# A segment-recurrent attention beside an MLP on one core: memory row subtracted, transposed scores in 128-token tiles, 512-token blocks, fixed instruction order

## The chip, the cores and the metric

One Trainium2 chip, one core of it. The metric is device microseconds (us) of one execution. Most executions of one kernel agree within 0.3%. All kernels quoted gave correct results.

Engine names as the profile has them: PE is TensorE (matmuls), PEld its weight loads, DVE is VectorE, ACT is ScalarE, POOL is GpSimd, SP is SyncE (here it only issues DMAs). A trailing q (SPq) is an engine's own queue. "L419" is line 419 of that kernel.

## The reference, cut to what matters

```python
x  = A_x                                   # [1, 2048, 1024] bf16
xn = layernorm(x)
return x + A(xn, ...) + B(xn, ...)

def A(x, mem0, Wq, Wk, Wv, Wo, seg_len):   # 64 segments of 32 tokens, 32 heads of 128, 8 memory rows
    mem = mem0
    for s in range(64):
        h = concat([mem, x[segment s]])                    # 40 rows
        q, k, v = h @ Wq, h @ Wk, h @ Wv
        p = softmax(mask(q @ k.T * scale))                 # memory rows and columns unmasked, rest causal
        o = (p @ v) @ Wo
        mem = o[:8]; outs.append(o[8:])                    # the next segment needs this one's memory
def B(x, w1, w2, w3, w4):
    h  = gelu(layernorm(x) @ w1)                           # 1024 -> 1024
    x1 = x + token_shift(h) @ w2                           # 1024 -> 1024
    return x1 + gelu(layernorm(x1) @ w3) @ w4              # 1024 -> 3584 -> 1024
```

Both kernels break the recurrence in the same way. After the first segment the eight memory rows of a segment are nearly equal, so one row per segment stands for all eight. All rows are guessed beforehand from segment means (the *speculation*), all segments are then computed in parallel, and at the end a *check* compares the computed memory rows with the guessed ones. Only if it fails does a slow serial loop run. It never ran here.

## The kernel before: the parts that the change and the argument touch

The stages in order: LayerNorm and w1 (first stage), w2 (second), w3 and w4 (third, with the speculation), attention with its output projection. A segment is 33 columns in attention: one copy of its memory row and 32 tokens. The memory key counts eight times by an additive 3.0 (a power of two) in the mask. Tiles hold three segments (99 columns), blocks twelve (396 columns).

```python
def attention(B, hg, QT, KTt, V):                       # four heads hg, one block
    for ti, (tok, T, msk) in enumerate(B["tiles"]):     # T = 99: three segments of 1 + 32
        for hh in range(4):
            nc.tensor.matmul(S3[:, hh, :], QT[:, hh, l0:l0 + T], KTt[:, hh, l0:l0 + T], start=True, stop=True)
        nc.vector.tensor_tensor(sm, S3, msk, op=ALU.add)            # 99 x 396
        nc.vector.tensor_reduce(mx, sm, op=ALU.max)
        nc.vector.tensor_tensor(sm, sm, mx, op=ALU.subtract)
        nc.scalar.activation(e, sm, ACTF.Exp, scale=LN2)
        nc.vector.tensor_reduce(ss, e, op=ALU.add)
        nc.vector.reciprocal(rs, ss)
        nc.vector.tensor_tensor(Pn, e, rs, op=ALU.mult)
        for hh in range(4):                                          # transpose on PE
            nc.tensor.matmul(T3[:, hh, :], Pn[:T, hh, :T], ident[:T, :T], start=True, stop=True)
        nc.scalar.copy(PT, T3)
        for hh in range(4):
            nc.tensor.matmul(O3[:, hh, :], V[:T, ti, ...], PT[:T, hh, :T], start=True, stop=True)
        nc.scalar.copy(oS[:, :, l0:l0 + T], O3)
# ... cut ...
for group in ((0,), (1,), (2,), (3,), (4, 5)):          # blocks of 12 segments, the last of 4
    for hg in range(8):
        # load wq, wk, wv (1 MB each); project Q, K over 396 columns, V over 384; attention
    out_proj(...)                                       # 32 matmuls of 512 columns per chain
```

The order of the instructions on each engine was left to the framework's scheduler: what stands after another in this text may run before it.

## Time and profile before

| | |
|---|---|
| time | 1677.18 us, median of 3 (1675.5 to 1679.21); 1676.58 with the fourth run that came with the result |
| span of the profiled run | 1674.9 us |
| first w3 matmul, first Q matmul | 163.1 us, 579.4 us |
| attention, first Q matmul to the end | 1095.5 us |

The first lines are from the page of the kernel before: busy time, share of the span and number of instructions by engine, then the share of each engine in the chain of work that ended last.

```profile
PE 1626.2 (97%) x10393; PEld 863.9 (52%) x10513; DVE 647.2 (39%) x1528; ACT 640.6 (38%) x1321; POOL 220.9 (13%) x380
...
PE 75%; DVE 10%; ACT 5%; DMA 4%; issue 3%; POOL 0%; SPq 0%; DVEq 0%; ACTq 0%; POOLq 0%
```

The next view tells for what PE waited: waiting line, releasing line, us in total, times, longest.

```profile
PE ps L233 <- ACT xn_160 L223: 10.9, 1, 10.9
PE ps L241 <- DVE xn2T L235: 5.4, 2, 4.3
PE psT L483 <- DVE Pn L479: 4.3, 14, 0.9
```

These waits add up to about 31 us, half of them at the start. The busy row leaves 48.7 us; the rest is the tail (5.8 us after PE's last matmul) and gaps too short for this view. In attention it waits 14 times for the softmax, never over 0.9 us. So PE's own instruction stream is the limit, and the question about any change is how many *slots* it takes from that stream. A busy PE hides this, because matmuls overlap: the mean record of a 512-column matmul is 379 ns long, yet one starts every 216 ns. Slots are read from starts. The following lines are from the timeline of PE: start, time from first start to last end, line, shapes, count.

```profile
519.27 1.29 PE L147 MATMUL ps<-xb,wv 128*128 128x71 bf16 x32
520.40 1.89 PE L338 MATMUL ps<-w_sb,h3T 128*128 128x512 bf16 x8
...
839.69 0.84 PE L419 MATMUL ps<-hTb,wk 128*128 128x396 bf16 x4
840.49 0.34 PE L489 MATMUL psO<-PT,V_7513 99*128 99x99 bf16 x4
840.83 0.39 PE L483 MATMUL psT<-c_ident_sb,Pn 99*99 99x99 bf16 x4
841.05 1.00 PE L419 MATMUL ps<-hTb,wk 128*128 128x396 bf16 x5
841.89 0.34 PE L489 MATMUL psO<-PT,V_7513 99*128 99x99 bf16 x4
842.07 1.51 PE L419 MATMUL ps<-hTb,wk 128*128 128x396 bf16 x8
843.42 5.34 PE L431 MATMUL ps<-wv,xTb 128*128 128x512 bf16 x23
```

Thirty-two matmuls of 71 columns take 520.40 - 519.27 = 1.13 us, so 35 ns each. From 839.69 to 843.42 are 3.73 us; 17 matmuls of 396 columns need 17 x 168 ns = 2.86 of them (168 ns is 10.75 us for 64 in a row), which leaves 73 ns for each of the 12 small ones of attention.

### The profile page before, as it was taken

Reading aid. Unit: us, or ns where it says so; the run is one execution under the profiler, and the core shown is the slowest. Engines: PE = TensorE matmul, PEld = TensorE weight load, DVE = VectorE, ACT = ScalarE, POOL = GpSimd, SP = SyncE. Lnnn points to the kernel's source line nnn. Section 1 sums busy time; section 2 is a strip of 40 time slices with the busy share of each in tenths; the row PEclk is TensorE's granted clock in tenths of the full one; section 3 lists DMA queues with packets and bytes.
Section 4 is the critical chain, followed back from the end, with each engine's and each line's share of the span. In section 5 each row is a group of like instructions: output and inputs, shape, how many; then the busy total and the mean of one; then the engine's idle time right before and its main releaser. Section 6 shows DMA issues by size and latency. Waiting matters only on the chain.

```text
span 1674.9 us, 26877 instructions
## 1 busy us (share of the span) xinstructions
PE 1626.2 (97%) x10393; PEld 863.9 (52%) x10513; DVE 647.2 (39%) x1528; ACT 640.6 (38%) x1321; POOL 220.9 (13%) x380
## 2 busy tenths in 40 slices
PE   6999999999999999999999999999999999999998
PEld 5544444444445455554555545554555546665643
DVE  8447000000101145552455505564255533465540
ACT  7635302112030044541455415553255514565520
POOL 4222011010200122220111101110011100101000
PEclk9999999999999999999999999999999999999999
DMA  6864421030309887552565526564365633445211
GB/s 243 327 201 166 176 65 62 32 95 1 120 7 341 301 293 244 175 173 72 178 189 178 165 86 194 178 190 141 116 193 172 183 95 118 138 129 152 65 45 46
DMA packets 202804, 252.95 MB, mean 151 GB/s; under 512 B 15691, under 2 KB 165400, under 8 KB 202672
## 3 DMA queue, kind: packets, MB, share of 16 engines
q1 hardware_dynamic: 186928, 217.25, 41.1%
q0 software_dynamic: 15744, 33.92, 5.7%
q8 instruction: 85, 1.39, 0.3%
q14 instruction: 47, 0.39, 0.1%
HBM read 204.11 MB, written 30.07 MB: 140 GB/s over the span
## 4 chain that ended last, share of the span: by engine, by line
PE 75%; DVE 10%; ACT 5%; DMA 4%; issue 3%; POOL 0%; SPq 0%; DVEq 0%; ACTq 0%; POOLq 0%
PE ps L419 16%; PE ps L431 13%; PE ps L317 11%; PE ps L362 11%; PE ps L338 11%; DVE Pn L479 3%; DVE ss L475 2%; PE psT L483 2%; PE psO L489 2%; PE ps L256 2%; ACT e L473 2%; PE psS L466 2%; DMA wv<-in_A_Wv_dram 1%; DVE sm L471 1%; DVE sm L468 1%
## 5 line engine op out<-in xcount | busy, mean ns | idle before, releaser
L419 PE MATMUL ps<-hTb,wk 128*128 128x396 bf16 (+2 forms) x1536 | 265.7, 313 | 0.0
L419 PE MATMUL ps<-hTb,wq 128*128 128x396 bf16 (+2 forms) x1536 | 263.5, 314 | 0.8 <-DVE Ro L339 0.8
L362 PE MATMUL ps<-wo_sb,oX 128*128 128x512 bf16 x998 | 226.4, 379 | 1.2
L431 PE MATMUL ps<-wv,xTb 128*128 128x512 bf16 x984 | 224.4, 379 | 2.1
L338 PE MATMUL ps<-w_sb,h3T 128*128 128x512 bf16 x876 | 194.9, 379 | 1.1
L317 PE MATMUL ps<-xn3T,w_sb 128*128 128x512 bf16 x876 | 193.3, 379 | 1.1
L468 DVE TENSOR_TENSOR sm<-psS,c_mask_reg_sb 99x396 f32<-99x396 f32 x160 | 87.4, 563 | 218.1 <-PE psS L466 218.1
L419 PEld LDWEIGHTS <-wq 128*128 128x128 bf16 x1536 | 133.7, 98 | 71.3 <-issue 1.1
L318 ACT ACTIVATE h3T<-ps 128x512 bf16<-128x512 f32 x112 | 66.6, 597 | 268.1 <-PE ps L317 213.7
L419 PEld LDWEIGHTS <-wk 128*128 128x128 bf16 x1536 | 131.4, 98 | 67.5
L431 PEld LDWEIGHTS <-xTb 128*128 128x128 bf16 x1024 | 99.9, 98 | 115.7
L362 PEld LDWEIGHTS <-oX 128*128 128x128 bf16 x1024 | 97.9, 98 | 112.1 <-DVE oX L492 1.6
L317 PEld LDWEIGHTS <-w_sb 128*128 128x128 bf16 x896 | 87.6, 98 | 105.2
L338 PEld LDWEIGHTS <-h3T 128*128 128x128 bf16 x896 | 86.9, 98 | 103.1
L432 ACT CAST Vp<-ps 128x512 bf16<-128x512 f32 x128 | 74.9, 585 | 151.4 <-PE ps L431 146.8
L485 ACT CAST PT<-psT 99x396 bf16<-99x396 f32 (+1 forms) x176 | 85.9, 488 | 63.4 <-PE psT L483 61.3
L475 DVE TENSOR_REDUCE ss<-e 99x4 f32<-99x396 f32 (+1 forms) x176 | 95.0, 545 | 23.4 <-ACT e L473 22.3
L479 DVE TENSOR_TENSOR Pn<-e,rs 99x396 bf16<-99x396 f32 (+1 forms) x176 | 97.7, 559 | 6.9 <-DVE rs L477 0.5
L473 ACT ACTIVATE e<-sm 99x396 f32<-99x396 f32 (+1 forms) x176 | 90.4, 529 | 23.7 <-DVE sm L471 19.6
L490 ACT CAST oS<-psO 128x396 bf16<-128x396 f32 (+1 forms) x176 | 85.3, 485 | 33.4 <-PE psO L489 31.5
L471 DVE TENSOR_TENSOR sm<-sm,mx 99x396 f32<-99x396 f32 (+1 forms) x176 | 94.0, 553 | 0.5
L470 DVE TENSOR_REDUCE mx<-sm 99x4 f32<-99x396 f32 (+1 forms) x176 | 91.9, 541 | 1.1
(651 smaller groups left out, 1428.8 us busy)
## 6 DMA issues: line engine op xcount, KB each, us to landing
wv<-in_A_Wv_dram SPq DMA_DIRECT2D x48, 1024.0 KB
wq<-in_A_Wq_dram SPq DMA_DIRECT2D x40, 1024.0 KB
wk<-in_A_Wk_dram SPq DMA_DIRECT2D x40, 1024.0 KB
xt<-in_A_x_dram SPq DMA_DIRECT2D x32, 256.0 KB
R_scratch<-Ro POOLq DMA_DIRECT2D x16, 512.0 KB, 5.0
wo<-in_A_Wo_dram SPq DMA_DIRECT2D x8, 1024.0 KB
Rt<-R_scratch SPq DMA_DIRECT2D x32, 256.0 KB
wo_sb<-in_A_Wo_dram SPq DMA_DIRECT2D x4, 2048.0 KB
```

Source lines behind the costliest of these rows:

```text
L317: nc.tensor.matmul(ps[:], w3_sb[:, k, f * P:(f + 1) * P], xn3T[:, k, tb * 512:(tb + 1) * 512], start=(k == 0), stop=(k == KT - 1))
L338: nc.tensor.matmul(ps[:], h3T[:, f, j * P:(j + 1) * P], w4_sb[:, f, ch * 512:(ch + 1) * 512], start=(f == 0), stop=(f == FT - 1))
L362: nc.tensor.matmul(ps[:], oX[:, h, gl * P:(gl + 1) * P], wo_sb[:, h, cc], start=(h == 0), stop=(h == H - 1))
L419: nc.tensor.matmul(ps[:, :nb], w[:, k, hh * P:(hh + 1) * P], B["hTb"][:, k, :nb], start=(k == 0), stop=(k == KT - 1))
L431: nc.tensor.matmul(ps[:], B["xTb"][:, k, m * P:(m + 1) * P], wv[:, k, :], start=(k == 0), stop=(k == KT - 1))
L468: nc.vector.tensor_tensor(sm[:T, :, :T], S3, msk[:].unsqueeze(1).to_broadcast((T, 4, T)), op=ALU.add)
L470: nc.vector.tensor_reduce(mx[:T, :], sm[:T, :, :T], axis=AX.X, op=ALU.max)
L471: nc.vector.tensor_tensor(sm[:T, :, :T], sm[:T, :, :T], mx[:T, :].unsqueeze(2).to_broadcast((T, 4, T)), op=ALU.subtract)
L473: nc.scalar.activation(e[:T, :, :T], sm[:T, :, :T], ACTF.Exp, scale=LN2)
L475: nc.vector.tensor_reduce(ss[:T, :], e[:T, :, :T], axis=AX.X, op=ALU.add)
L479: nc.vector.tensor_tensor(Pn[:T, :, :T], e[:T, :, :T], rs[:T, :].unsqueeze(2).to_broadcast((T, 4, T)), op=ALU.mult)
L485: nc.scalar.copy(PT[:T, :, :T], T3)
```

## The change

Its intent: fewer and better shaped matmuls in attention, and an order of instructions set by hand. The parts of the rewrite:

- **The memory row is subtracted.** Keys and values are projected from x minus the segment's memory row (`xm`). Subtracting one vector from all keys of a segment changes no softmax; the memory key's score becomes 0, its weight is the constant 8 in the denominator, and its value is added back afterwards. The 33rd column of K and V goes away.
- **Scores are computed transposed** (keys on partitions), so that the weights go straight into the value matmul: no transpose on PE. The 32x32 diagonal blocks are transposed on DVE for the sum and back. The row's maximum is no longer subtracted before the exponential.
- **Tiles of 128 tokens and blocks of 512:** every big matmul has 512 columns.
- **Fixed order** (`manual_schedule`): each step (four heads of one block) is twelve chains of eight 512-column matmuls, and the attention of the step before hangs between the chains, three chains apart.
- The speculation's weights stream through the third stage; most transposes of the first two stages go through DMA; the check is turned round to 70 columns.

```diff
-        def proj_T(B, w, dst, scale):   # 396 columns
+    def k_chain(s, hh):                 # 512 columns of xm = x minus memory row
+            for k in range(KT):
+                nc.tensor.matmul(ps[:, 0:c], w[:, k, hh * P:(hh + 1) * P], xm[:, k, h2 * c:(h2 + 1) * c], ...)
+    def scores(s, m):
+        for hh in range(4):             # weights K (128 columns), 132 columns of Q: 4 x (32 tokens + 1 memory)
+            nc.tensor.matmul(ps[:, hh, 0:TW], s.K[:, hh, m * P:(m + 1) * P], s.Q[:, hh, m * TW:(m + 1) * TW], start=True, stop=True)
+        for j in range(4):
+            nc.scalar.activation(ET[q, :, :], ps[q, :, W * j:W * (j + 1)], ACTF.Exp, scale=SCALE)
+        nc.vector.transpose(EQ[:, :, 0:SEG], ET[:, :, 0:SEG])
+        nc.vector.tensor_tensor(EQ, EQ, causal, op=ALU.mult)
+        nc.vector.tensor_reduce(ss, EQ[:], axis=AX.X, op=ALU.add)
+        nc.vector.reciprocal(rs[:], ss)
+        nc.vector.tensor_tensor(Pn[:], EQ[:, :, 0:SEG], rs, op=ALU.mult)
+        for j in range(4):
+            nc.vector.transpose(BD[q, :, W * j:W * j + SEG], Pn[q, :, :])
+            nc.gpsimd.tensor_copy(BD[q, :, W * j + SEG:W * (j + 1)], ET[q, :, SEG:W])
+    def values(s, m):
+        for hh in range(4):
+            nc.tensor.matmul(ps[:, hh, 0:TW], s.V[:, m, hh * P:(hh + 1) * P], BD[:, hh, :], start=True, stop=True)
+        nc.vector.tensor_tensor(oX[...], p4[...], VM[...], op=ALU.add)      # memory value added back
+        nc.scalar.copy(oTm[...], p4[:, :, :, SEG])
+# ... cut: first segment, output chains ...
+    def normalise(b):                   # once a block: memory columns divided by their sums
+        nc.vector.tensor_scalar(r3, p3_, float(M), None, op0=ALU.add)
+        for j in range(4):
+            nc.vector.reciprocal(r3[:, j, :], r3[:, j, :])
+        nc.vector.tensor_tensor(o4, o4, r3, op=ALU.mult)
+        nc.vector.tensor_tensor(oTm[:, :, z], oTm[:, :, z], VM[:, :, z], op=ALU.add)
+# ... cut ...
+    for i in range(NS + 1):             # the fixed order
+        if s.hg == 0 and s.b > 0:
+            make_xm(s.b)                # eight DVE subtractions of [128, 512]
+        if pp is not None:
+            at(0, values, pp, 3)        # at(c, ...): right after chain c of this step
+        if p is not None and not last:
+            at(0, scores, p, 0)
+            for m in range(3):
+                at(3 * m + 3, values, p, m)
+                at(3 * m + 3, scores, p, m + 1)
+        if s.hg == 1 and s.b > 0:
+            for c in range(8):
+                at(0, out_chain, s.b - 1, c)
+        if s.hg == 2 and s.b > 0:
+            at(2, normalise, s.b - 1)
+        # ... chains 0 to 11 (Q, K, V), each followed by what hangs on it ...
+        if last:
+            # ... out_chain 0 and 1, normalise, out_chain 2 to 4 ...
+            verify()                    # 256 matmuls, a DVE/ACT chain, 4 matmuls, the flag
+            for c in range(5, 8):
+                out_chain(s.b, c)
```

## The prediction

> **What bounds the kernel now.** TensorE. The page's busy row gives PE 97% of 1674.9 us; the chain that ended last is 75% PE; the waits view shows PE idle for about 31 us; the table of windows shows PE 96 to 99.5% in every stretch from 200 to 1600 us. So the change pays only through matmul slots. Slots, from start-to-start spacing in timeline and chain: 512 columns 216 ns (10.79 us for 50), 396 columns 168 ns (10.75 us for 64), 71 columns 35 ns (32 in 1.13 us), a 99-column attention matmul about 73 ns (12 among 17 projections that need 2.86 of 3.73 us). Counts times slots give 1629 us, within 3% of the span.
>
> **Removed.**
> - Attention: 22 tiles x 32 heads x 3 (scores, transpose, values) = 2112 x 73 ns = 154 us.
> - Q and K over 2119 columns (64 copies of the memory row included): 461.
> - Wide matmuls for the memory rows' V and the check, 128 x 216 ns: 28.
> - Transposes and spreading matmuls of the first stages, 384 x about 60 ns: 23.
> - Speculation: 23.
>
> **Added.**
> - Transposed scores and values: 1024 matmuls of 132 columns, estimated from the slots above at 60 to 65 ns: 64 us. Their weights have 128 columns; the Trainium skill, "TensorE: Matmul & The Clock Gate", section "Weight-path perf modes", ties fast weight load to that, and the trace agrees: 95 to 98 ns for 128 columns, 123 to 130 for 99.
> - Q and K in 512-blocks, 2048 x 216 ns: 442, plus 1.5.
> - Memory-row projections 512 x 35 ns: 18; first segment 6; check 9; speculation 18; segment sums and 32 transposes 7; normalising 1.
>
> V (221), output (221) and the MLP matrices (498) stay. New sum about 1510 us, 120 less.
>
> **Critical path.** Nearly all of it, since PE is the limit. Given back as new PE waits in the fixed order (estimates): start 14 and tail 6; first stage (DVE about 2.9 us a tile against 3.45 on PE, transposes through DMA) 8; three block borders (transposed load of 1 MB, then eight DVE subtractions ahead of the softmax) 9; the check, whose last matmuls stand before three output chains and wait for a DVE/ACT chain, 7; attention hooks of three chains (5.2 us) against a softmax chain of about 4.2 us, 10; end and first segment 7. Sum 1571; I shade it to 1565.
>
> PREDICTION: 1565 us, 1530 to 1625. Faster by over 2%: 0.92; within 2%: 0.05; slower: 0.03.
>
> **What would show it.** PE matmul records near 9,500 instead of 10,393; 132-column matmuls near 60 ns start to start; steady steps near 23 us; block period near 240 us; the MLP's wide part starting near 142 us instead of 163, attention near 560 instead of 578; PE above 95%; PE's waits naming the softmax's last copies, the block's transposed load and the check.
>
> **What would make it wrong.** No run here shows a DMA transpose. The Trainium skill, "DMA: Bandwidth & Descriptors", section "Latency and other measured facts", gives 261 GB/s: an estimate of 1 us per 256 KB tile, 4 us per 1 MB block. If a tile takes over 3.4 us, the first two stages become DMA-bound (up to +60 us) and the borders stall. If the softmax chain (exponentials on quarters, small POOL copies) exceeds 5.2 us, each of 128 units stalls. If small matmuls cost 90 ns, +30 us.

## The result, and the profile after

| | before | after |
|---|---|---|
| median of 4 runs | 1676.58 us (1675.5 to 1679.21) | 1608.34 us (1605.74 to 1615.02) |
| ratio, 95% interval | | 0.9596 (0.9574 to 0.9619): faster |
| span of the profiled run | 1674.9 us | 1613.2 us |
| first w3 matmul | 163.1 us | 156.0 us |
| first Q matmul | 579.4 us | 562.3 us |
| attention, first Q matmul to the end | 1095.5 us | 1050.9 us |

The profiled run of the changed kernel is its slowest: 1615.02 us, 6.7 above its median.

The changed kernel is 68 us faster where 111 were predicted. First what came as foreseen: the busy row of the changed kernel's page.

```profile
PE 1527.0 (95%) x9278; PEld 779.9 (48%) x9404; DVE 622.4 (39%) x1689; ACT 510.0 (32%) x1305; POOL 266.5 (17%) x890
```

PE lost 99 us of busy time, and 9278 matmul records are close to the foreseen 9500. Its timeline in a steady stretch (columns as before):

```profile
909.74 0.40 PE L566 MATMUL psO<-BD,V 128*128 128x132 bf16 x4
909.98 0.39 PE L540 MATMUL psS<-Q,K 128*128 128x132 bf16 x4
910.21 5.34 PE L511 MATMUL psK<-xm,w 128*128 128x512 bf16 x23
915.39 0.40 PE L566 MATMUL psO<-BD,V 128*128 128x132 bf16 x4
...
932.32 0.40 PE L566 MATMUL psO<-BD,V 128*128 128x132 bf16 x4
```

A step is 932.32 - 909.74 = 22.58 us. Twelve chains of 8 x 216 ns are 20.7 of them, so the 32 small matmuls take 58 ns each, the foreseen "near 60". A unit (three chains, four value and four score matmuls) is 5.65 us, with no wait. The slots were right. Then PE's waits:

```profile
PE psO L566 <- DVE BD L557: 20.4, 7, 4.3
PE psT L213 <- DVE xn L207: 16.0, 3, 8.0
PE psC L690 <- DVE chk L688: 6.3, 1, 6.3
PE ps L232 <- DMA xn2T<-xn: 6.2, 2, 3.6
PE psO L566 <- ACT oTm L574: 6.0, 4, 2.4
PE ps L273 <- DVE x L274: 6.0, 3, 4.8
PE psS L540 <- ACT ET L544: 3.8, 2, 2.7
```

Where the old kernel waited 14 times for at most 0.9 us in attention, the new one waits for the softmax's last copies (BD) only seven times, but for up to 4.3 us. The fixed order cannot put other matmuls there. Two of these places, first by the timeline of DVE. This is the third step of a block, where `normalise` stands:

```profile
879.13 1.25 DVE L557 STREAM_TRANSPOSE BD<-Pn 32x128 bf16<-32x128 bf16 x4
880.41 0.69 DVE L631 TENSOR_SCALAR rm<-psN 128x512 f32<-128x512 f32 x1
881.14 3.39 DVE L633 RECIPROCAL rm<-rm 128x128 f32<-128x128 f32 x4
884.56 1.05 DVE L636 TENSOR_TENSOR oTm<-oTm,rm 128x512 bf16<-128x512 bf16 x1
...
886.27 0.68 DVE L570 TENSOR_TENSOR oX<-psO,VM 128x512 bf16<-128x512 f32 x1
888.27 0.31 DVE L546 STREAM_TRANSPOSE EQ<-ET 128x128 f32<-128x128 f32 x1 [1.31 <-ACT ET L544]
...
1016.61 4.91 DVE L402 TENSOR_TENSOR xm<-xT,MZ 128x512 bf16<-128x512 bf16 x8
1021.43 0.68 DVE L570 TENSOR_TENSOR oX<-psO,VM 128x512 bf16<-128x512 f32 x1
```

DVE keeps the order of the program here: the value matmuls that the addition into oX (L570) reads had ended at 881.4 us, but it starts at 886.27, when the 5.9 us of normalising (from 880.41) are over. The softmax of the next tile starts that much later, by way of ACT: its copy into oTm waited 5.19 us for this addition, and the exponentials stand behind that copy. At 1016.61, a block border, eight subtractions of `make_xm` do the same for 4.9 us. PE at the same two places (the number in brackets is the wait before the line):

```profile
881.48 5.34 PE L511 MATMUL psK<-xm,w 128*128 128x512 bf16 x24
891.11 0.41 PE L566 MATMUL psO<-BD,V 128*128 128x132 bf16 x4 [4.29 <-DVE BD L557]
...
1017.45 5.34 PE L501 MATMUL psQ<-xT,w 128*128 128x512 bf16 x23
1026.28 0.62 PE L566 MATMUL psO<-BD,V 128*128 128x132 bf16 x4 [3.48 <-DVE BD L557]
1026.69 0.65 PE L540 MATMUL psS<-Q,K 128*128 128x132 bf16 x4
1027.13 7.79 PE L511 MATMUL psK<-xm,w 128*128 128x512 bf16 x24
```

Look at what follows the wait of 3.48 us. Twenty-four K matmuls take 7.79 us; the same 24 before the wait of 4.29 us took 5.34. The table of windows (busy time of PE, PEld, DVE, ACT and POOL with counts, then granted clock as a share of full TensorE speed, DMA share, GB/s) tells why:

```profile
1026.00:1028.00 2.00, 1.72 (x11) 1.18 (x12) 0.91 (x2) 0.34 (x2) 0.00 (x0) 0.50 0.80 272
1030.00:1032.00 2.00, 2.00 (x6) 0.76 (x5) 1.62 (x6) 0.58 (x1) 0.00 (x0) 0.50 0.00 0
1034.00:1036.00 2.00, 2.00 (x17) 1.15 (x15) 0.69 (x1) 0.66 (x2) 0.00 (x0) 1.00 0.00 0
```

At 1030 us PE is fully busy, yet only six matmul records touch these 2 us (17 at 1034 us, eight of them small), and the granted clock is 0.50. So a wait of a few us has a second bill, read from starts: about 2.8 us here (2.4 in the K matmuls, 0.4 in the eight small ones), 1.7, 2.5 and 2.5 us after the three normalisings, 1.9 us after the check. The Trainium skill, "TensorE: Matmul & The Clock Gate", section "Why this matters for your kernels", advises to leave no PE-idle gap over about 3 us between bursts, else the clock falls to half. This trace agrees: the wait of 3.48 us is followed by 0.50. But a wait of 2.0 us at 163 us was followed by 0.52 (165 to 168 us) too, so staying just under 3 us is not safe here.

### The profile page after: what moved, and what is told of

The parts are those of the page before. It is cut to its first block, busy times and chain, and to the rows that moved or that the text cites. A ratio compares the mean times of both kernels' runs of the same rounds, so it can differ in the third digit from the quotient of the medians.

```text
span 1613.2 us, 23770 instructions
## 1 busy us (share of the span) xinstructions
PE 1527.0 (95%) x9278; PEld 779.9 (48%) x9404; DVE 622.4 (39%) x1689; ACT 510.0 (32%) x1305; POOL 266.5 (17%) x890
## 3 DMA queue, kind: packets, MB, share of 16 engines
q1 hardware_dynamic: 183152, 181.44, 37.8%
## 5 line engine op out<-in xcount | busy, mean ns | idle before, releaser
L511 PE MATMUL psK<-xm,w 128*128 128x512 bf16 (+1 forms) x1256 | 242.0, 345 | 1.4 <-issue 0.2
L501 PE MATMUL psQ<-xT,w 128*128 128x512 bf16 x996 | 231.7, 380 | 2.7 <-ACT Q L502 1.2
L518 PE MATMUL psV<-w,xm 128*128 128x512 bf16 x999 | 232.8, 383 | 1.3
L653 PE MATMUL psP<-wo_sb,oX 128*128 128x512 bf16 x1003 | 224.7, 384 | 1.4 <-issue 0.3
L558 POOL CAST BD<-ET 32x4 bf16<-32x4 f32 x512 | 99.8, 195 | 589.3 <-ACT ET L544 571.9
L456 PE MATMUL ps<-w,h3T 128*128 128x512 bf16 x874 | 193.7, 380 | 1.1
L511 PEld LDWEIGHTS <-w 128*128 128x128 bf16 x1280 | 124.1, 100 | 91.3 <-issue 10.6
L557 DVE STREAM_TRANSPOSE BD<-Pn 32x128 bf16<-32x128 bf16 x512 | 155.6, 304 | 9.6
L501 PEld LDWEIGHTS <-w 128*128 128x128 bf16 x1024 | 97.6, 98 | 111.3 <-issue 1.5
L544 ACT ACTIVATE ET<-psS 32x132 f32<-32x132 f32 x512 | 138.7, 271 | 9.3
L570 DVE TENSOR_TENSOR oX<-psO,VM 128x512 bf16<-128x512 f32 (+1 forms) x128 | 87.4, 683 | 124.7 <-PE psO L566 124.2
L438 PE MATMUL ps<-xn3T,w3a 128*128 128x512 bf16 x448 | 99.5, 384 | 2.0 <-ACT h3T L439 2.0
```

Source lines behind the costliest of these rows:

```text
L438: nc.tensor.matmul(ps[:], w3[:, k, (f % FH) * P:(f % FH + 1) * P], xn3Ts[tb][:, :, k, :], start=(k == 0), stop=(k == KT - 1))
L456: nc.tensor.matmul(ps[:], h3T[:, f, j * P:(j + 1) * P], w4t[f // 4][:, f % 4, ch * 512:(ch + 1) * 512], start=(f == 0), stop=(f == FT - 1))
L501: nc.tensor.matmul(ps[:], w[:, k, hh * P:(hh + 1) * P], xT[:, k, :], start=(k == 0), stop=(k == KT - 1))
L511: nc.tensor.matmul(ps[:, 0:c], w[:, k, hh * P:(hh + 1) * P], xm[:, k, h2 * c:(h2 + 1) * c], start=(k == 0), stop=(k == KT - 1))
L518: nc.tensor.matmul(ps[:], xm[:, k, m * P:(m + 1) * P], w[:, k, :], start=(k == 0), stop=(k == KT - 1))
L544: nc.scalar.activation(ET[q, :, :], ps[q, :, W * j:W * (j + 1)], ACTF.Exp, scale=SCALE)
```

## The experiments

Theory A: what is missing against the prediction is mostly one-off work on DVE that the fixed order puts ahead of a softmax (and the check's chain ahead of output chains); PE waits for it and then also runs slow. Rivals: the softmax chain is too long by itself (B); the loss lies in the first two stages (C); the lowered clock is no cost of its own (D). Savings below are differences of ratios times 1676 us. Beside them stands the attention part of each trace (first Q matmul to the end), which repeats well: 1050.9, 1052.2, 1050.8 and 1050.6 us in the four traces in which it was untouched. The early stages scatter by some us from run to run, so this part is the sharper measure. The first four runs were made on one chip, the others on a second one; each call measured the kernel before anew, and the ratios refer to that.

### The repeat

> The changed kernel again, unaltered, as the reference for the other three on this chip: 1603 to 1615 us, ratio to the kernel before 0.957 to 0.963. Every theory expects that.

Measured: 0.9606 (0.958 to 0.9632), median 1612.28 us. As expected.

### Normalising where DVE is idle

```diff
             for c in range(8):
                 at(0, out_chain, s.b - 1, c)
-        if s.hg == 2 and s.b > 0:
-            at(2, normalise, s.b - 1)
+                if c == 3:
+                    at(0, normalise, s.b - 1)
```

> Only the place of the normalising of the memory columns is changed: from the softmax stretch of the third head group to between the fourth and fifth output chain of the second head group, where DVE has nothing else to do. Theory A (a one-off DVE batch ahead of the softmax makes PE wait, and PE then runs some us at a lowered clock): the three waits of 4.3, 4.0 and 4.0 us for the last BD copy disappear, and with them about 2 us each of slow matmuls: 1608 - 18 = 1590 us, at least 14 saved. Rival B (the waits come from a softmax chain that is simply too long for its three chains, whatever else DVE does): waits stay at the same places or move, under 4 us saved. Rival C (what is missing against the prediction lies in the first two stages): under 4 us saved here.

Measured: 0.9459 (0.9439 to 0.9479), 24.6 us less than the repeat; attention 1031.4 us, 20.8 less. PE's waits now:

```profile
PE psO L566 <- DVE BD L557: 8.0, 4, 3.5
```

The three waits are gone (20.4 to 8.0 us, 12.4 us); the other 8.4 us of the 20.8 have no wait to be charged to. The slow matmuls account for them: by the trace's record of the granted clock, the half-clock stretches of attention cost 7.9 us less than in the repeat. Not an instruction was removed. Rival B falls: the steady softmax chain is fast enough.

### Useless matmuls in the waits

```diff
+    def fill(n, w, x):
+        ps = mm_tile("psF")
+        for _ in range(n):
+            nc.tensor.matmul(ps[:], w, x, start=True, stop=True)
 ...
+                    if s.b > 0 and s.hg == 2 and m == 1:
+                        at(6, fill, 18, A["k", s.i][:, 0, 0:P], xm[:, 0, 0:512])
+                    if s.b > 1 and s.hg == 0 and m == 0:
+                        at(3, fill, 15, A["q", s.i][:, 0, 0:P], xT[:, 0, :])
                     at(3 * m + 3, values, p, m)
 ...
+        fill(28, wo_sb[:, 0, 0:P], oX[:, 0, :])          # ahead of the check's last matmuls
```

> Useless matmuls of 512 columns are put where PE waits: 18 ahead of the values after each normalising (three places), 15 ahead of the values at the two later block borders, 28 ahead of the check's last matmuls: 97 matmuls more, 21 us of PE work, sized to a little less than the waits. The waits themselves remain. Theory A (the lowered clock after a wait costs 2 to 3 us by itself): faster by 3 x 2 + 2 x 2.9 + 2 = 13 us, about 1595, and the windows after these places show a granted clock of 1.00. Rival D (the clock figure is only a record of idleness and costs nothing after it): the same time as the repeat, within 3 us, or slower.

Measured: 0.9521 (0.9508 to 0.9534), 14.2 us less than the repeat with 24 us more of matmuls; attention 1035.9 us, 16.3 less. (The edit adds 3 x 18 + 2 x 15 + 28 = 112 matmuls, and the trace has 112; the 97 of the expectation were miscounted.) The stretch that holds one normalising and one border, in the repeat:

```profile
860.00:1050.00 190.00, 182.22 (x997) 89.48 (x996) 111.12 (x324) 86.98 (x239) 33.05 (x158) 0.96 0.45 137
```

and with the filling:

```profile
860.00:1050.00 190.00, 189.34 (x1056) 93.23 (x1054) 110.59 (x320) 86.39 (x238) 33.58 (x159) 1.00 0.45 138
```

The granted clock goes from 0.96 to 1.00. Rival D falls: the lowered clock is worth about 14 us by itself, here bought back without shortening a single DVE chain.

### The check's last matmuls later

```diff
         chk = ...                                # DVE and ACT work as before
-        pc = mm_tile("psC")
-        nc.tensor.matmul(pc[...], qones[...], chk[:], ...)   # and what follows, to the flag
+    def verify_count():                          # the same, on its own
 ...
             for c in range(5, 8):
                 out_chain(s.b, c)
+                if c == 6:
+                    verify_count()
```

> Only the check's last four matmuls and the flag are moved from before the last three output chains to before the last one. Theory A: the wait of 6.3 us for the check's DVE and ACT chain goes, and about 2 us of slow matmuls after it: 8 us saved, about 1600. Rival E (the DVE chain of the check then delays the output chains' additions, or the flag comes too late for the end): under 3 us saved.

Measured: 0.9549 (0.9526 to 0.9572), 9.6 us less; attention 1043.2 us, 9.0 less. The wait for chk is no longer among PE's waits. Rival E falls.

### The border's subtraction in pieces

```diff
-        if s.hg == 0 and s.b > 0:
-            make_xm(s.b)                          # eight on DVE, [128, 512]
+        # piece m: [128, 8 x 128] of token tile m, once the old block's value chain m has read it
+                if s.hg == 0 and s.b > 0:
+                    at(0, xm_piece, s.b, 2, nc.vector)
+                early = s.hg == NHG - 1 and s.b + 1 < NB
+                    if early and m == 2:
+                        at(9, xm_piece, s.b + 1, 0, nc.vector)
+                if early:
+                    at(9, xm_piece, s.b + 1, 1, nc.gpsimd)
+                    at(11, xm_piece, s.b + 1, 3, nc.gpsimd)
```

A second buffer for x and xm was not tried.

> Only the subtraction of the memory row at the three block borders is changed: instead of eight DVE operations at the head of the new block's first step, four pieces by token tile, two on POOL and two on DVE, begun as soon as the old block's value chains have read their columns. Theory A: the border waits (3.5, 3.5 and about 1.1 us for the last BD copy) go, and with the first two about 2.9 us each of slow matmuls: 12 to 14 us saved, about 1596. Rival B (softmax chain too long by itself): the waits stay. Rival F (the border is bound by the transposed load of 1 MB, whose landing took 6 to 11 us): PE waits for the load or for the pieces instead, under 4 us saved.

Measured: 0.951 (0.9497 to 0.9523), 16 us less than the repeat; attention 1035.1 us, 17.1 less. PE at the border of 1012 us now:

```profile
1012.16 0.41 PE L575 MATMUL psO<-BD,V 128*128 128x132 bf16 x4 [0.95 <-DVE BD L566]
```

The wait is 0.95 us. Rival F falls: the transposed load of 1 MB, issued in the old block's last step, is in time.

### Five buffers for x1

```diff
-                x1 = ring.tile([P, D], F32, tag="x1")
+                x1 = ring.tile([P, D], F32, tag="x1", bufs=5)
```

> Only the buffers of x1 in the second stage go from 3 to 5. In the four traces of the changed kernel's first two stages so far, the second stage (first w2 matmul to first w3 matmul) took 57 to 65 us where its matmuls need 55.3, and PE waited 1.3 to 6.0 us for DVE, which waited for the store of an old x1. Theory G (too few buffers for a store that lands late): that wait goes, stage at most 57.5 us, 0 to 8 us saved in all, mean 4. Rival H (DMA is saturated there, so stores fall behind whatever the buffers): the wait stays or moves to the transposed tiles.

Measured: 0.9627 (0.9613 to 0.964), not faster. The second stage ran without a wait, 55.6 us (57.3 to 64.6 in the traces with three buffers and DMA transposes), and PE then waited here:

```profile
PE ps L438 <- ACT h3T L439: 8.7, 1, 8.7
```

The third stage grew from 404.6 us in the repeat to 412.9, and both stages together took 468.5 us against 466.5. The wait moved. Theory G named the wait rightly and the cause wrongly; rival H remained. Here the removed wait came back further on, because something else limited the chain.

### Transposes of the second stage on PE again

```diff
-                nc.sync.dma_start_transpose(xn3Ts[n // 4][:, n % 4, :, :], xn3[:])
+                if n < NT - 2:
+                    pend[n] = xn3
+                else:
+                    nc.sync.dma_start_transpose(xn3Ts[n // 4][:, n % 4, :, :], xn3[:])
+                if n - 2 in pend:
+                    pe_transpose(n - 2, pend.pop(n - 2))     # 8 matmuls, 2 ACT copies
```

> In the second stage 14 of the 16 tiles are transposed on PE again (8 matmuls of 128 columns and two ACT copies each, two tiles late), only the last two through DMA. Rival H (DMA transposes saturate the DMA engines there): the mean DMA share in this stage falls from about 1.0 to under 0.6, the x1 stores land sooner than their 5.7 to 6.4 us, and DVE's wait for them goes. Cost: 112 matmuls x 58 ns = 6.5 us of PE. Net: second stage about 62 us, whole time within 4 us of the unchanged 1608 to 1612. If transposes are cheap for DMA, the share hardly falls and the kernel is 6 us slower.

Measured: 0.9634 (0.962 to 0.9647). The DMA view of the second stage (86 to 146 us) with DMA transposes and five buffers: of SP's queue the packets, MB and share of the 16 engines' time; of the stores the count, KB each and median us to landing:

```profile
q1 hardware_dynamic: 11678, 6.31, 56.7%
...
R_scratch<-x POOLq DMA_DIRECT2D x15, 512.0 KB, 8.4
```

and with PE transposes:

```profile
q1 hardware_dynamic: 1056, 3.67, 16.2%
...
R_scratch<-x POOLq DMA_DIRECT2D x14, 512.0 KB, 3.0
```

The queue's share falls from 56.7 to 16.2%, the mean DMA share from 0.93 to 0.46, and a store lands in 3.0 instead of 8.4 us: rival H holds, the DMA engines are nearly full in this stage, and the transposes fill them. (This kernel has three x1 buffers and the other one five; the repeat, with three buffers and DMA transposes, shows a share of 0.90 and 6.1 us in the same window, so the buffers are not what made the difference.) In both windows the queue moved w3's second half (3.67 MB); the other 2.64 MB are some ten transposed tiles, and they took (56.7 - 16.2)% of 60 us = 24 us of all engines, 2.4 us for 256 KB, 109 GB/s. That is the price in a crowded stage: the two tiles that this run still sends through DMA, in a quieter stretch (148 to 156.5 us, DMA share 0.66), took 33.0% of 8.5 us, so 1.4 us each, 187 GB/s. The time did not change: the transposes' 6.5 us came back to PE, and it waited 5.0 us more for an ACT copy at the stage's end. The second stage took 66.9 us, not the expected 62.

### All mends together

```diff
+ normalise among the output chains; check's count before the last chain; border in pieces; five x1 buffers
+ last step: scores and values three chains (later one output chain) apart, not two:
+            values(s, 0); scores(p, 3); out_chain(s.b, 0)
+            values(p, 3); scores(s, 1); out_chain(s.b, 1)
+            values(s, 1); scores(s, 2); out_chain(s.b, 2)
+            values(s, 2); scores(s, 3); out_chain(s.b, 3)
+            values(s, 3); out_chain(s.b, 4); normalise(s.b); out_chain(s.b, 5)
+            verify(); out_chain(s.b, 6); verify_count(); out_chain(s.b, 7)
-        nc.gpsimd.dma_start(out_v[...], ot[:])
+        (nc.sync if b == NB - 1 else nc.gpsimd).dma_start(out_v[...], ot[:])
```

> All together: normalising among the output chains, the check's count before the last chain, the border in pieces, five x1 buffers, the last step with attention units three chains or one output chain apart instead of two, and the last block's stores issued from SP. Theory A, adding up: 1610 - 25 (normalising, measured) - 10 (check, measured) - 13 (border) - 10 (last step: waits of 6.0 and 3.8 us and slow matmuls after them) - 4 (x1) - 3 (tail) = 1545, range 1538 to 1560. If the waits merely move, under 50 us saved: above 1560.

Measured: 0.927 (0.9255 to 0.9284), median 1553.52 us, 56 us less than the changed kernel. That is 8.5 us over the expected 1545 and inside the range: the 4 us for x1 did not come, and moving the normalising gives 20.8 us in attention rather than the 25 added up. Attention is 992.5 us, 59.7 less than in the repeat. The single savings there (20.8 + 9.0 + 17.1) are 46.9 of it; the last step and the store from SP are the rest. From the last DVE addition's end to the end of the span are 5.0 us, 8.9 in the changed kernel, so about 3.9 of the 12.8 us that remain lie in the tail; neither part of the edit was run alone.

> The kernel with all of the first mends again, unaltered, as the reference for the next two on this chip: 1550 to 1557 us. Every theory expects that.

Measured: 0.926 (0.9227 to 0.9293), median 1553.95 us. As expected. PE waited 10.0 us at the third stage's start in this trace.

### w3's second half later

```diff
-                if n in (3, 7):
-                    kk = slice(0, 4) if n == 3 else slice(4, 8)
-                    nc.sync.dma_start(w3b[:, kk, :], w3_v[:, kk, FH * P:F])
+                if n == NT - 1:
+                  for kk in (slice(0, 4), slice(4, 8)):
+                    nc.sync.dma_start(w3b[:, kk, :], w3_v[:, kk, FH * P:F])
```

> On top of it, only the two loads of w3's second half (3.6 MB) are moved from the midst of the second stage to behind its last transposed tile; they are needed 24 us after the third stage's start. With five x1 buffers the wait in the second stage had gone and come back as one of 5.9 to 8.7 us at the start of the third, where ACT waits for the transposes of old tiles. Theory H (DMA is saturated in the second stage: from the share with and without DMA transposes, 1.00 against 0.45, 12 transposes in 55 us cost about 2.5 us of all engines each): the load's 9 us leave the stage, the wait at the third stage's start falls under 1.5 us and with it about 2 us of slow matmuls: 6 to 8 us saved, about 1546. Rival I (ACT's order alone makes that wait: the last tile's chain through DVE, POOL and ACT stands ahead of the first evacuation): wait over 4 us, under 2 us saved.

Measured: 0.9203 (0.9188 to 0.9218), 9.6 us less than the mended kernel; the wait at the third stage's start is 1.3 us. Second and third stage together take 459.6 us instead of 471.1. Rival I falls. This is where the wait that had moved really came from: a bulk load ahead of the transposes in a stage whose DMA engines are full.

### First loads in another order

```diff
             load_x(1)
-            nc.sync.dma_start(w1_sb[:, :, 0:512], w1_v[:, :, 0:512])
             load_x(2)
             load_x(3)
+            nc.sync.dma_start(w1_sb[:, :, 0:512], w1_v[:, :, 0:512])
 ...
-                if gi == 3:                # w2; w3's first half at gi 4 and 5
+                if gi == 4:                # w2; w3's first half at gi 5, behind the last transpose
```

> On top of that, the first four x tiles are loaded ahead of w1, and w2 and the first half of w3 are asked for after the transposes of the first stage instead of between them. PE's waits before 60 us were 16.3 us for the normalised tiles and 5.7 us for transposed tiles. Theory H: the second falls under 2 us and the first by about 3 us, with 1 to 3 us of slow matmuls: 5 to 10 us saved on the previous one, about 1538. Rival J (the first stage is bound by DVE's 3.2 us or more a tile): the first transposes come earlier but stage two starts at the same time, under 3 us saved.

Measured: 0.9177 (0.9161 to 0.9193), median 1539.29 us; 4.4 us less than the one before, with intervals that overlap slightly. So rival J, which allows under 3 us, is not clearly excluded; the second stage did start earlier, at 85.5 us (92.1 in the run before, 86.8 to 92.1 in all others of the changed kernel's line). The expectation is missed in part: PE's waits for normalised tiles went from 16.7 to 14.0 us and for transposed ones from 6.0 to 4.0, not under 2. This is the fastest version: 8.2% under the kernel before. Its longest waits:

```profile
PE psT L213 <- DVE xn L207: 14.0, 3, 7.8
PE ps L232 <- DMA xn2T<-xn: 4.0, 1, 4.0
PE psO L574 <- DVE BD L565: 3.2, 3, 1.3
PE ps L446 <- ACT h3T L447: 1.3, 1, 1.3
...
```

PE is 98% busy with a mean clock of 0.999 (0.980 in the changed kernel).

### Score matmuls doubled

```diff
+            for _ in range(2):
-            nc.tensor.matmul(ps[:, hh, 0:TW], s.K[:, hh, m * P:(m + 1) * P], s.Q[...], start=True, stop=True)
+              nc.tensor.matmul(ps[:, hh, 0:TW], s.K[:, hh, m * P:(m + 1) * P], s.Q[...], start=True, stop=True)
```

> The changed kernel of the case with each score matmul issued twice (the second overwrites the first with the same values): 512 matmuls of 132 columns more. Theory (the attention of the changed kernel is bound by PE's slots, 58 ns for such a matmul in the timeline): 512 x 58.4 ns = 30 us more, about 1640. Rival (the softmax chain paces it): under 10 us more, or far more than 30 because each of 128 chains now misses its turn.

Measured: 0.9719 (0.9683 to 0.9756), 18.9 us more than the repeat; attention 1070.9 us, 18.7 more. Neither figure was met. The steady pitch is as the theory has it:

```profile
935.74 0.40 PE L567 MATMUL psO<-BD,V 128*128 128x132 bf16 x4
...
941.61 0.40 PE L567 MATMUL psO<-BD,V 128*128 128x132 bf16 x4
```

A unit takes 5.87 us instead of 5.65, so four more matmuls cost 0.22 us and 128 units about 28 us. But PE's waits for BD shrank from 20.4 to 17.9 us and for oTm from 6.0 to 4.5, and the K matmuls after the two later borders took 6.7 and 6.2 us where the kernel before this edit had 7.8 and 7.7. Extra work that falls on a waiting engine costs less than its slots: part of it fills waits, and shorter waits leave fewer slow matmuls behind, as the table shows.

### All savings in attention, from two figures of each trace

The trace records the granted clock as stretches of 1.00 and 0.50; in the changed kernel's attention each stretch of 0.50 lasted 3.41 or 6.83 us. Half of PE's busy time within such stretches is an estimate of what they cost. With PE's idle time between matmuls, this accounts for every run (us, attention only, against the repeat with 37.8 idle and 19.7 lost to half clock; the other traces with this part untouched have 18.2 to 18.4 lost):

| run | idle time gone | half-clock cost gone | work added, tail | sum | measured |
|---|---|---|---|---|---|
| normalising elsewhere | 12.5 | 7.9 | | 20.4 | 20.8 |
| useless matmuls | 24.0 | 16.8 | 112 x 216 ns = 24.2 added | 16.6 | 16.3 |
| check later | 6.3 | 2.7 | | 9.0 | 9.0 |
| border in pieces | 8.1 | 8.6 | | 16.7 | 17.1 |
| all mends | 34.6 | 19.7 | 3.9 of tail gone | 58.2 | 59.7 |
| doubled scores | 4.7 | 5.9 | 512 x 58 ns = 29.7 added | -19.1 | -18.7 |

The useless matmuls took the place of about as much idle time, so that run gained by the clock alone. With all mends no half-clock stretch is left in attention before PE's last matmul.

## Why the prediction was right or wrong, point by point

- **PE is the limit, and slots are what counts: right.** Small matmuls 58 ns (60 to 65 foreseen), steady step 22.6 us (23), third stage 404 to 409 us (387 + 18 foreseen), matmul records 9278 (9500). PE's share, foreseen above 95%, was 94.7%, and a block took about 249 us from border to border (1026.28 to 1275.56 us, the values after the border's wait) instead of 240: about 13 of them are the waits at one border and one normalising with the slow matmuls after them.
- **The time: inside the range, 43 us over the number.** The saving was 68 us instead of 111. The step that failed is the list under "Critical path" of what is given back.
- **"Attention hooks ... against a softmax chain ... 10": wrong place.** In steady units PE waits nothing. What was overlooked is `normalise`: 5.9 us of DVE ahead of a softmax, three times. The prediction has it with 1 us of PE time and with no wait; moving it was worth 21 to 25 us.
- **"Three block borders 9": mechanism right, size short.** The subtractions ahead of the softmax were named. The waits for BD were 8.1 us in all (3.5, 3.5 and 1.1), near the 9. Taking the subtractions away saved 16 to 17 us, because the slow matmuls after the waits come on top. The transposed load, named with it, was no problem.
- **"The check ... 7": right**, 6.3 us of wait; with the slow matmuls after it 9 to 10.
- **Every wait was priced at its length.** That is the general error. The lowered clock after the waits cost another 14 to 16 us in attention, shown by filling the waits with useless work (16.8 us of it in that trace's clock record).
- **"First stage 8", nothing for the second: short by 3 to 14 us.** The third stage began at 156.0 instead of 142 us in the first trace, at 144.6 to 150.5 in four. The estimate of 1 us for a DMA transpose of 256 KB was low; 1.4 us were measured in a quiet stretch and 2.4 in the crowded second stage, and the stage's stores and bulk loads came on top. So rival C holds for this part of the loss, and for this part alone. "If a tile takes over 3.4 us, the first two stages become DMA-bound" put the threshold too high, since it left out the other traffic.
- **"Attention near 560": met (562.3), but by an error.** The prediction's own figures give 142 + 405 = 547; the number written down does not follow from any sum on record. That it was met is luck: the early stages took longer than foreseen.
- **"Tail 6, as before": short.** 8.9 us from the last addition to the end against 5.1 us before.

Still open: how much of the 12.8 us that the mended kernel gained beyond the single edits belongs to the last step and how much to the stores from SP, since only the 3.9 us of the tail can be read off; which of the two reordered groups of loads gave the last 4.4 us; and what the first stage's remaining 14 us of waits for DVE could give.

## What to carry to other kernels

When instruction order is fixed by hand, list all one-off work of each in-order engine (per block, per phase, at the end) and ask what stands behind it: a batch of 5 us on a 40% busy engine stopped a 97% busy one, and moving it to where that engine idles cost nothing. Price a PE wait of 3.5 us and more at its length plus the 1.7 to 2.8 us of lowered clock that were seen here. Whether several short waits are better than a long one was not tested: in the changed kernel's attention, waits of up to 1.4 us that stood alone were followed by no half clock, but a row of 1.2, 1.1 and 2.7 us in the last step was. When a wait is removed and the time stays, look for the same microseconds at the next stage before trying another buffer; here it was a bulk load that could come later.

## What the Trainium skill lacked or had wrong

- "Advanced Engine Details and Errata", section "X-Bar Transpose (TRN2)", says that transposing DMAs are as fast as regular ones, and "DMA: Bandwidth & Descriptors", section "Latency and other measured facts", gives 261 GB/s. Here SBUF-to-SBUF transposes of 256 KB took 1.4 us of all engines each in a quiet stretch (187 GB/s) and about 2.4 us in a crowded one (some 109 GB/s), where a neighbouring store of 512 KB landed in 8.4 us instead of 3.0.
- "TensorE: Matmul & The Clock Gate", section "Back-to-back issue gap", gives 81 ns for 128 columns and 131 ns for 512 as sustained rates of weight load and matmul pairs. Here such pairs ran at 58 ns for 132 columns and 216 ns for 512, which fits the formula that the section keeps for an isolated matmul, N / 2.4 + 2.5 ns (an estimate from it: 57.5 and 215.8 ns).
- The same page, section "HAM oscillation — how this bites in real kernels", prices an idle gap for one kernel of short bursts: 1.67 us at the lowered clock each, half of it lost. Inside this busy kernel a gap cost more: 1.7 to 2.8 us of lost PE time after a wait of 3.5 to 6.3 us, and filling the gaps with useless matmuls gained 14 us of 1610.
